# Sums of the attention and memory parts: the 13 that GpSimd made are made by VectorE at the same places

## The chip, the cores and the metric

The kernel runs on one core of a Trainium2 chip. A core has a matrix engine (TensorE, PE in the profile; its weight loads are PEld), a vector engine (VectorE, DVE), a scalar engine (ScalarE, ACT), a general engine (GpSimd, POOL) and a queue engine that issues the DMA transfers (SyncE, SP). Each works through its own list of instructions in order; semaphores tie the lists together. SBUF is the memory on the chip that all engines use, PSUM the eight banks into which PE writes. The metric is the time of one execution on the device in microseconds, the median of several runs.

## The reference

Two layers follow each other twice, on 2048 tokens of width 512: an attention layer with a memory, and a gated feed-forward layer. Both add to the tokens `x`.

```python
# attention: 32 heads of width 16, N = 4 segments of L = 512 tokens
q, k, v = x@wq, x@wk, x@wv              # x here is the layer norm of the tokens
for s in range(4):
    logits = einsum('bhqd,bhkd->bhqk', qs, ks) * scale + mask
    a_dot = einsum('bhqk,bhkd->bhqd', softmax(logits), vs)
    num = einsum('bhld,bhde->bhle', phi(qs), M)
    den = einsum('bhld,bhd->bhl', phi(qs), z)[..., None] + 1e-6
    o = g * num / den + (1 - g) * a_dot       # g = sigmoid(beta), one per head
    M, z = M + phi(ks)^T vs, z + sum(phi(ks))
x = x + concat(o) @ wo
# feed-forward, F = 1792
x = x + (gelu(norm(x) @ w_gate) * (norm(x) @ w_up)) @ w_down
```

`phi(t)` is `t + 1` above zero and `exp(t)` below. What this document is about is the sum in `o`: the attention part `(1 - g) * a_dot` plus the memory part `g * num / den`. In the first segment of each of the two attention layers the memory is empty and there is no sum.

## The kernel before

The work is cut into 8 steps `k`, four segments in each of the two rounds of layers. All weights and the tokens (`x_sb`) stay in SBUF. A step's work runs through the engines as follows. The names are those of tiles in the profile.

- PE makes `q`, `k` and `v` from the transposed, normalised tokens `xnT`; the results are copied out of PSUM (`ps`) to `q`, `kf`, `vaug`. `kx` holds masked copies of `kf`.
- PE makes scores (`ps<-q,kf`, `ps<-q,kx`); ACT takes the exponential into `pt` (L1864); the causal mask is laid on `pt` by POOL (L1813, and L1818 in two halves) or by DVE (L1823, a product with the triangle `tri`).
- PE multiplies `pt` with the values (`vaug`, `vz`). DVE turns the result round into `byq` (L1391), inverts the denominators `r` (L1401), scales to `ab` (L1407) and turns back into `aT` (L1414). `aT` now holds the attention part of one block of 8 heads: 128 rows by 512 tokens, bf16.
- For the memory, PE multiplies `phiq` with the state `mblk`; DVE scales to `am` (L1226); a DMA on SP's queue transposes `am` into `amT`. The state is kept in `macc` and `zacc` and spread into `mblk` by DVE (L1303, L1305, L1286). `phiq` and the keys' counterpart come from an exponential on ACT (L1147), a minimum `e` on DVE or POOL (L1170) and a sum on DVE (L1151).
- `aT` and `amT` are added into `aT` (L1417). This is the line that is changed. There are four blocks a segment and six segments with a memory, so 24 such sums.
- PE multiplies `aT` with `wo_sb`; DVE adds to `x_sb` (L1463), takes mean and variance (`st`, `mv`), and DVE or POOL normalises into `xn` (L920); a DMA transposes to `xnT`.
- The feed-forward part: `wg_sb`, gelu on ACT into `gel_sb`, `wu_sb`, the product on DVE (L1557), `wd_sb`, and a sum into `x_sb` (L1463).

The order of all this is worked out while the program is built. A planner keeps a clock for each engine, posts jobs with a time at which they are ready and a slack, and writes the instructions of each engine out in the order in which its clocks serve them. Some jobs may go to either of two engines: `on_dve_or_pool` (L712) posts such a job on DVE and, with a further slack, on POOL; the first of the two that is free takes it. The slack is `at_pool` for these sums and differs by stretches of 20 us of the planner's clock. In the built program POOL gets 13 of the 24 sums and DVE 11. The job's body, `add`, is handed the engine that took it.

Before a sum is posted, its `aT` must have been turned back and its `amT` must have landed by the planner's clock (`kept`, `put`). The instruction itself waits for the DMA's semaphore and for DVE's. After it stand the `wo_sb` products, which read `aT`, and the next step's `amT`, which reuses the tile.

Of the kernel before, what the change touches and what calls it, by code (L numbers as in the profile page):

```python
# [11 lines left out]
ALU = mybir.AluOpType  # L12
# [560 lines left out]
def order(pol, nc, cst, seg, wrk, psp, A_x, A_wq, A_wk, A_wv, A_wo, A_beta, B_x, B_w_gate, B_w_up, B_w_down, out):  # L573
# [138 lines left out]
    def on_dve_or_pool(ready, slack, later, fast, slow, emit, told):  # L712

        taken = []
        ck.dve.post(ready, slack, (fast, lambda: emit(nc.vector), told), taken=taken)
        if later is not None:
            ck.pool.post(ready, slack + later, (slow, lambda: emit(nc.gpsimd), told), taken=taken)
# [268 lines left out]
    class Att:  # L986
# [360 lines left out]
        def flush_item(self, flush, masked):  # L1347
            k = self.k
            u, b, h, n, pars, used = flush
# [6 lines left out]
            c0, c1 = (0, L) if h is None else (half * h, half * h + half)  # L1356
# [21 lines left out]
            def done():  # L1378
                for t in used:
                    slot = places[t]  # L1380
                    slot_users[slot] -= 1
                    if not slot_users[slot]:
                        slot_free[slot] = ck.made()
                flushed.append(number)
                if last:
                    ev["flushed", k] = ck.pe

                def turn():
                    if n == 0:
                        self.byq = wrk.tile([P, 2, TPS * 4, 32], F32, tag="byq", bufs=1, name="byq")  # L1390
                    nc.vector.transpose(out=(self.byq[:, pars[0], :, :].rearrange("p a c -> p (a c)") if h is None else  # L1391
                                             self.byq[:].rearrange("p u a c -> p (u a c)")[:, 0:2 * na * 32]), in_=ps()[:])

                def byq():
                    if h is None:
                        return self.byq[:]
                    return self.byq[:].rearrange("p u a c -> p (u a c)")[:, 0:2 * na * 32].rearrange("p (u a c) -> p u a c", u=2, c=32)

                def inverse():
                    self.r = wrk.tile([P, 2, TPS * 4, 1], F32, tag="pvr", bufs=1, name="r")  # L1400
                    nc.vector.reciprocal(out=self.r[:, :, 0:na, :], in_=byq()[:, :, :, DH:DH + 1])  # L1401

                made = []

                def scale():
                    made.append(seg.tile([P, TPS * 4, 32], BF16, tag=f"ab{unit % 2}", bufs=1, name="ab"))
                    nc.vector.tensor_tensor(out=made[0][:, 0:na, :].rearrange("p a (u d) -> p u a d", u=2),  # L1407
                                            in0=byq()[:, :, :, 0:DH],
                                            in1=self.r[:, :, 0:na, :].to_broadcast([P, 2, na, DH]), op=ALU.mult)

                def back():
                    if not self.aT:
                        self.aT = seg.tile([P, KT, L], BF16, tag="aT", bufs=1, name="aT")
                    nc.vector.transpose(out=self.aT[:, b, c0:c1], in_=made[0][:, 0:na, :].rearrange("p a c -> p (a c)"))  # L1414

                def add(eng):
                    eng.tensor_tensor(out=self.aT[:, b, c0:c1], in0=self.aT[:, b, c0:c1], in1=self.amT[b][:, c0:c1], op=ALU.add)  # L1417

                part = (c1 - c0) / L

                def turned(t):
                    on_dve_or_pool(t, slack, pol.at_pool, Port(0.15 + 0.275 * part), Port(0.16 + 1.0 * part, True), add, there)

                def there(t):
                    ev["turned", unit] = t
                    for i in range(2):
                        if h in (None, i):
                            ev["aTh", k, i, b] = t
                            self.halves[b] += 1
                    if self.halves[b] == 2:  # L1430
                        ev["aT", k, b] = t

                def kept(t):
                    ck.when(lambda: (k == 0 or ("wo", k - 1) in ev) and (self.s == 0 or ("amT", k, b) in ev), put)

                def put():
                    ck.dve.post(ck.pe, slack, (0.146 + 0.56 * part, back, turned if self.s else there))

                steps = [(0.71, turn, ps.read)]
                if 1 in pars:  # L1440
                    steps += [(0.155 + 0.2 * part, inverse, None), (Port(0.142 + 0.55 * part), scale, kept)]
                ck.dve.post(ck.made(), slack, *steps)
# [564 lines left out]
```

## Time and profile before

| | us |
|---|---|
| median of 3 runs | 536.3 (536.02 to 536.4) |
| the profiled execution, its own time | 536.81 |
| its span, first to last instruction | 535.1 |
| PE busy / DVE busy / ACT busy / POOL busy | 525.1 / 433.7 / 445.9 / 268.1 |

The granted clock of PE is 1.00 over the span. A row of the timeline is: start, duration, engine, line, operation, what is written and read, shape, how many are merged, and in brackets how long the engine sat idle before it and what ended that. A row of the chain of waits is start, duration and what. Instructions of one engine overlap a little at their ends, so the time that one takes from its engine is best read from its start to the next one's start.

### The profile page before, as it was taken

To read this page: it belongs to the slowest core of one execution; us is meant where nothing else is said; L and a number is where in the kernel's file an instruction comes from. 1 tells how busy PE (TensorE), PEld (TensorE's weight loads), DVE (VectorE), ACT (ScalarE), POOL (GpSimd) and SP (SyncE) were. 2 spreads that over 40 slices of the span, in tenths; PEclk is the share of its full clock that TensorE was granted. 3 is DMA by queue.
4 is the path that set the end of the run, shared out by engine and by line. 5 is a ranking of instruction groups with operands and counts; after the bars stand their busy time and mean duration, and the time that the engine had idled before them with its cause. 6 is when DMAs were issued, how large, how long until landed. Compare 5 with 4: busy or idle time off the path is not lost.

```text
span 535.1 us, 24177 instructions
## 1 busy us (share of the span) xinstructions
PE 525.1 (98%) x10697; PEld 276.3 (52%) x10697; DVE 433.7 (81%) x823; ACT 445.9 (83%) x598; POOL 268.1 (50%) x333
## 2 busy tenths in 40 slices
PE   9999989998999999999999999999999999999997
PEld 4454455444545454555564544555555456555554
DVE  6899996999997999879987788888977997586342
ACT  6999989887999989899898899799989988952320
POOL 2986472568541966528773366491654354500000
PEclk9999999999999999999999999999999999999999
DMA  8366940323231232201221113310260132102101
GB/s 268 76 121 139 215 141 4 69 41 73 44 60 24 49 55 42 33 12 25 51 44 31 25 24 32 61 34 1 52 103 3 33 51 52 24 2 51 33 2 41
DMA packets 76762, 29.99 MB, mean 56 GB/s; under 512 B 61042, under 2 KB 76658, under 8 KB 76658
## 3 DMA queue, kind: packets, MB, share of 16 engines
q1 hardware_dynamic: 76368, 28.20, 26.0%
q8 instruction: 83, 1.36, 1.0%
q10 hardware_dynamic: 290, 0.26, 0.1%
q14 instruction: 21, 0.17, 0.1%
HBM read 9.70 MB, written 2.10 MB: 22 GB/s over the span
## 4 chain that ended last, share of the span: by engine, by line
PE 77%; DVE 4%; ACT 3%; POOL 1%; issue 1%; DMA 0%; ACTq 0%
PE ps L541 77%; ACT pt L1864 1%; ACT gel_sb L1616 1%; POOL kx L726 1%; DVE xn L920 1%; ACT gel_sb L1519 1%; POOL e L1170 1%; ACT gel_sb L779 0%; DMA xnT<-xn 0%; DVE x_sb L1463 0%; DVE st L856 0%; DVE mblk L1286 0%; DVE byq L1391 0%; DVE x_sb L869 0%; ACT L1519 0%
## 5 line engine op out<-in xcount | busy, mean ns | idle before, releaser
L1864 ACT ACTIVATE pt<-ps 128x1024 bf16<-128x1024 f32 x288 | 278.9, 1036 | 26.8 <-PE ps L541 19.9
L1813 POOL TENSOR_SCALAR_AFFINE_SELECT pt<-pt 128x256 bf16<-128x256 bf16 (+1 forms) x192 | 113.6, 604 | 148.0 <-ACT pt L1864 145.6
L541 PE MATMUL ps<-xnT,wg_sb 128*32 128x512 bf16 (+3 forms) x1367 | 107.7, 362 | 0.3 <-DMA xnT<-xn 0.3
L541 PE MATMUL ps<-wd_sb,gel_sb 128*32 128x512 bf16 (+2 forms) x1431 | 106.1, 354 | 0.0
L541 PE MATMUL ps<-xnT,wu_sb 128*32 128x512 bf16 (+1 forms) x1252 | 103.6, 379 | 0.2 <-ACT gel_sb L1519 0.2
L1557 DVE TENSOR_TENSOR gel_sb<-gel_sb,ps 128x512 bf16<-128x512 bf16 x112 | 75.2, 683 | 30.8 <-PE ps L541 28.5
L541 PEld LDWEIGHTS <-gel_sb 128*32 128x32 bf16 (+1 forms) x1623 | 53.2, 97 | 41.2 <-issue 2.2
L541 PEld LDWEIGHTS <-wu_sb 128*32 128x32 bf16 (+1 forms) x1252 | 45.8, 97 | 45.3 <-issue 2.0
L541 PEld LDWEIGHTS <-wg_sb 128*32 128x32 bf16 (+1 forms) x1367 | 47.5, 97 | 38.7 <-issue 1.5
L1391 DVE STREAM_TRANSPOSE byq<-ps 128x512 f32<-128x512 f32 x64 | 45.4, 710 | 24.5 <-PE ps L541 23.8
L1170 POOL TENSOR_SCALAR e<-e 128x512 bf16<-128x512 bf16 x32 | 50.0, 1565 | 7.1 <-ACT e L1147 6.4
L1463 DVE TENSOR_TENSOR x_sb<-x_sb,ps 128x512 bf16<-128x512 bf16 (+1 forms) x54 | 34.0, 635 | 17.8 <-PE ps L541 17.7
L1818 POOL TENSOR_SCALAR_AFFINE_SELECT pt<-pt 64x1024 bf16<-64x1024 bf16 x32 | 38.1, 1192 | 17.8 <-ACT pt L1864 15.6
L541 PE MATMUL ps<-xnT,wk_sb 128*32 128x512 bf16 (+2 forms) x330 | 34.9, 377 | 0.7 <-ACT pt L1864 0.7
L541 PE MATMUL ps<-pt,vaug 128*32 128x256 bf16 (+2 forms) x1344 | 35.1, 239 | 0.1
L541 PE MATMUL ps<-wv_sb,xnT 128*32 128x512 bf16 (+1 forms) x227 | 32.4, 380 | 2.2 <-DVE x_sb L1463 1.8
L541 PE MATMUL ps<-xnT,wq_sb 128*32 128x512 bf16 (+2 forms) x339 | 34.0, 377 | 0.0
L1616 ACT ACTIVATE gel_sb<-gel_sb 128x1024 bf16<-128x1024 bf16 (+4 forms) x31 | 33.3, 1157 | 0.0
L541 PE MATMUL ps<-q,kx 32*128 32x64 bf16 (+2 forms) x1120 | 31.4, 217 | 0.6 <-ACT pt L1864 0.3
L541 PEld LDWEIGHTS <-vaug 128*32 128x32 bf16 x1344 | 27.2, 97 | 9.2 <-issue 1.6
L856 DVE BATCH_NORM_STATS2 st<-x_sb 128x6 f32<-128x512 bf16 x46 | 31.2, 679 | 0.4
L541 PEld LDWEIGHTS <-kx 32*128 32x128 bf16 x1120 | 16.8, 92 | 28.1 <-issue 27.4
(128 smaller groups left out, 722.1 us busy)
## 6 DMA issues: line engine op xcount, KB each, us to landing
vz<-vaug SPq DMA_DIRECT2D x14, 136.0 KB, 3.0
wg_sb<-in_B_w_gate_dram SPq DMA_DIRECT2D x8, 224.0 KB, 4.0
wu_sb<-in_B_w_up_dram SPq DMA_DIRECT2D x8, 224.0 KB, 3.9
wd_sb<-in_B_w_down_dram SPq DMA_DIRECT2D x7, 256.0 KB, 5.7
x_sb<-in_A_x_dram SPq DMA_DIRECT2D x3, 512.0 KB, 6.5
out_dram<-x_sb SPq DMA_DIRECT2D x12, 128.0 KB, 1.9
xnT<-xn SPq DMA_TRANSPOSE x56, 2.5
kx<-kf SPq DMA_DIRECT2D x12, 64.0 KB, 3.3
```

The costliest lines, as they stand in the source:

```text
L541: self.nc.tensor.matmul(*args, **kw)
L726: return lambda: eng.tensor_scalar(out=kx[:, :, C * which:C * which + n], in0=kf[:, :, 0:n], scalar1=masks[:, which:which + 1], scalar2=No ...
L856: nc.vector.bn_stats(out=self.st6[:, 0, :], in_=x_sb[:, self.tt0 + j, :])
L920: eng.tensor_scalar(out=xn[:], in0=x_sb[:, self.tt0 + j, :], scalar1=self.mv[:, j, 1:2] if self.wide else self.mv[:, j, 0:1], scalar2=self ...
L1170: lambda eng: eng.tensor_scalar(out=e[0][:], in0=e[0][:], scalar1=1.0, scalar2=None, op0=ALU.min), summed)
L1391: nc.vector.transpose(out=(self.byq[:, pars[0], :, :].rearrange("p a c -> p (a c)") if h is None else self.byq[:].rearrange("p u a c -> p ...
L1463: ck.dve.post(ck.made(), slack, (0.15 + 0.00104 * (c1 - c0), lambda: nc.vector.tensor_tensor(out=xt, in0=xt, in1=ps()[:, 0:c1 - c0], op=AL ...
L1557: ck.dve.post(ck.made(), NORMAL, (0.683, lambda: nc.vector.tensor_tensor(out=g, in0=g, in1=ps()[:], op=ALU.mult), lambda t: (ps.read(t), e ...
L1616: return (0.205 + 0.427 * (f1 - f0), lambda: nc.scalar.activation(out=g, in_=g, func=ACT.Gelu_apprx_tanh), lambda t: self.gelu_done(t, f0, ...
L1813: nc.gpsimd.affine_select(out=view, in_=view, pattern=[[0, 4], [0, n], [1, C]], compare_op=ALU.is_ge, fill=0.0, base=C, channel_multiplier=-1)
L1818: nc.gpsimd.affine_select(out=view, in_=view, pattern=[[0, 4 * TPS], [1, C]], compare_op=ALU.is_ge, fill=0.0, base=0, channel_multiplier=-1)
L1864: nc.scalar.activation(out=pt_all[:, s0:s0 + 2, 2 * p:2 * p + 2, :].rearrange("p r h c -> p h r c"), in_=ps_all[:, pair[0]:pair[1] + 1, :] ...
```

## The change

The body of the sum no longer uses the engine that it is handed, but always VectorE:

```diff
                 def add(eng):
-                    eng.tensor_tensor(out=self.aT[:, b, c0:c1], in0=self.aT[:, b, c0:c1], in1=self.amT[b][:, c0:c1], op=ALU.add)
+                    nc.vector.tensor_tensor(out=self.aT[:, b, c0:c1], in0=self.aT[:, b, c0:c1], in1=self.amT[b][:, c0:c1], op=ALU.add)
 
                 part = (c1 - c0) / L
```

The planner still books 13 of the sums on POOL's clock, so that every other instruction keeps its place in its engine's list. A sum that was booked on POOL is written into DVE's list behind what DVE had been given by then. Semaphore waits that named POOL name DVE instead. The lists of PE, ACT and SP are the same as before but for those waits.

The following rows show an engine's list in order; the shapes are written with their inner dimensions (`128x4x128` is 128 rows of 512). First POOL, at two sums of the second segment's four blocks (near 115 to 128 us in the profile). Before:

```order
L1813 AFFINE_SELECT pt<-pt 128x4x128
L1417 TENSOR_TENSOR aT<-aT,amT 128x512
L1170 TENSOR_SCALAR e<-e 128x512
L1813 AFFINE_SELECT pt<-pt 128x4x64 x2
L1813 AFFINE_SELECT pt<-pt 128x4x128
L920 TENSOR_SCALAR xn<-x_sb,mv,rs 128x512
L1813 AFFINE_SELECT pt<-pt 128x4x64 x2
L894 TENSOR_SCALAR ve<-mv 128x2
L899 TENSOR_TENSOR rs<-ve,mhalf 128x2
L1813 AFFINE_SELECT pt<-pt 128x4x128
L1417 TENSOR_TENSOR aT<-aT,amT 128x512
L1818 AFFINE_SELECT pt<-pt 64x1024 x2
```

And with the change:

```order
L1813 AFFINE_SELECT pt<-pt 128x4x128
L1170 TENSOR_SCALAR e<-e 128x512
L1813 AFFINE_SELECT pt<-pt 128x4x64 x2
L1813 AFFINE_SELECT pt<-pt 128x4x128
L920 TENSOR_SCALAR xn<-x_sb,mv,rs 128x512
L1813 AFFINE_SELECT pt<-pt 128x4x64 x2
L894 TENSOR_SCALAR ve<-mv 128x2
L899 TENSOR_TENSOR rs<-ve,mhalf 128x2
L1813 AFFINE_SELECT pt<-pt 128x4x128
L1818 AFFINE_SELECT pt<-pt 64x1024 x2
```

The minimum `e` and the half-masks of L1818 now follow a mask directly; the sums ahead of them are gone from this list.

DVE at the first of these two sums (near 115 us):

```order
 L1407 TENSOR_TENSOR ab<-byq,r 128x2x16x16
 L1414 STREAM_TRANSPOSE aT<-ab 128x512
+L1417 TENSOR_TENSOR aT<-aT,amT 128x512
 L1463 TENSOR_TENSOR x_sb<-x_sb,ps 128x512
 L1823 TENSOR_TENSOR pt<-pt,tri 128x1024
```

The sum stands right behind the transpose that makes its input, and ahead of a sum into `x_sb` and a mask product.

DVE near 395 us, in the third segment of the second attention layer:

```order
 L1414 STREAM_TRANSPOSE aT<-ab 128x512
 L1463 TENSOR_TENSOR x_sb<-x_sb,ps 128x512
+L1417 TENSOR_TENSOR aT<-aT,amT 128x512
 L1463 TENSOR_TENSOR x_sb<-x_sb,ps 128x256
 L1823 TENSOR_TENSOR pt<-pt,tri 128x1024
 L1414 STREAM_TRANSPOSE aT<-ab 128x512
 L1226 TENSOR_TENSOR am<-ps,rdm 128x512
+L1417 TENSOR_TENSOR aT<-aT,amT 128x512
 L1463 TENSOR_TENSOR x_sb<-x_sb,ps 128x256
 L778 CAST gel_sb<-ps 128x512
```

Two sums come in within a few instructions, each ahead of a half sum into `x_sb`.

## The prediction

> **What bounds the kernel now.** I read the page first, then the chain of waits, the waits of TensorE (PE) alone, the moved line, and last the timeline at the places where the moved instruction will stand.
>
> ```profile
> PE 525.1 (98%) x10697; PEld 276.3 (52%) x10697; DVE 433.7 (81%) x823; ACT 445.9 (83%) x598; POOL 268.1 (50%) x333
> 356.06 175.83 PE ps L541 x3787
> PE ps L541 <- DVE x_sb L1463: 1.8, 1, 1.8
> ```
>
> PE is busy for 525.1 of 535.1 us, and the chain runs on PE alone for the last 175.83 us of matmuls. A gain can come only from PE's few waits; the longest is one of 1.8 us, for VectorE (DVE). A loss comes wherever DVE becomes late for PE by more than PE's margin there. As hardly any wait is left to swallow it, I carry such lateness through to the end in full.
>
> ```profile
> L1417 POOL TENSOR_TENSOR aT<-aT,amT x13: 1152/1155/1165, 102.0 to 455.1; 128x512 bf16<-128x512 bf16 x13
> L1417 DVE TENSOR_TENSOR aT<-aT,amT x11: 383/615/1353, 101.7 to 481.0; 128x512 bf16<-128x512 bf16 x11
>   PEld L541: 0.2, 1
> ```
>
> Of the 24 sums, 13 run on GpSimd (POOL) at 1.155 us each, 15.0 us together; 11 run on DVE already. PE's weight loads idled behind a sum once, for 0.2 us. So the sums do not bound the kernel where they are. What counts is what their absence frees on POOL and what their presence delays on DVE.
>
> **The change part by part.** Removed: 13 POOL instructions. Added: the same 13 on DVE. PE, ACT and the DMA queue keep their order. Five of the 13 land where DVE has no idle time: one each at 102.0 (place A), 115.8 (B) and 126.5 (C), two at 395.4 and 398.0 (D). The other eight land at 155.6, 224.1, 225.7, 230.2, 339.4, 408.3, 422.5 and 453.5. The sum rows of two tables by stretch follow, first the four stretches of 3 us from A, B, C and D's first sum, then the eight stretches of 4 us from the other places (two of these overlap).
>
> ```profile
> sum 12.00, PE 12.00 PEld 5.81 DVE 11.96 ACT 9.38 POOL 11.01; mean PE 3.00 PEld 1.45 DVE 2.99 ACT 2.35 POOL 2.75
> sum 32.00, PE 32.00 PEld 17.05 DVE 25.91 ACT 30.18 POOL 18.67; mean PE 4.00 PEld 2.13 DVE 3.24 ACT 3.77 POOL 2.33
> ```
>
> In the eight, DVE is idle for 6.09 of 32 us, 0.76 a place, in gaps in which it waits for PE's products. A sum of about 0.35 us (next fence) fits into that, so I cost these eight at nothing. The cover is DVE's own idle time; were it gone, each place could cost up to 0.35 us.
>
> Place A first, with the price of one sum on DVE:
>
> ```profile
> 101.69 0.38 DVE L1417 TENSOR_TENSOR aT<-aT,amT 128x512 bf16<-128x512 bf16 x1
> 102.00 0.68 DVE L1557 TENSOR_TENSOR gel_sb<-gel_sb,ps 128x512 bf16<-128x512 bf16 x1
> 103.20 0.67 DVE L1557 TENSOR_TENSOR gel_sb<-gel_sb,ps 128x512 bf16<-128x512 bf16 x1
> 104.11 0.40 PE L541 MATMUL ps<-q,kx 32*128 32x64 bf16 x12
> 131.40 0.04 issue
> ```
>
> From a sum's start to the next instruction's is 102.00 - 101.69 = 0.31 us; by duration it is 0.38. I take 0.31 where the next instruction overlaps its end as here. PE's score matmul at 104.11 writes into the bank that the product of 103.20 reads until 103.87; 0.04 passes between a release and the start (the row of the chain). The margin is 104.11 - 103.87 - 0.04 = 0.20, so PE is late by 0.31 - 0.20 = **+0.1 us**, at most 0.2.
>
> Place B:
>
> ```profile
> 114.41 0.63 ACT L1147 ACTIVATE e<-q 128x512 bf16<-128x512 bf16 x1
> 115.08 0.71 DVE L1414 STREAM_TRANSPOSE aT<-ab 128x512 bf16<-128x512 bf16 x1
> 115.72 0.65 DVE L1463 TENSOR_TENSOR x_sb<-x_sb,ps 128x512 bf16<-128x512 bf16 x1
> 115.88 1.15 POOL L1417 TENSOR_TENSOR aT<-aT,amT 128x512 bf16<-128x512 bf16 x1 [0.30 <-DVE aT L1414]
> 116.29 1.29 DVE L1823 TENSOR_TENSOR pt<-pt,tri 128x1024 bf16<-128x1024 bf16 x1
> 116.97 0.40 PE L541 MATMUL ps<-q,kx 32*128 32x256 bf16 x12
> 117.00 1.93 POOL L1170 TENSOR_SCALAR e<-e 128x512 bf16<-128x512 bf16 x1
> 117.76 0.29 PE L541 MATMUL ps<-pt,vz 128*32 128x64 bf16 x16
> ```
>
> POOL has been free since 115.58 (idle for 0.30 before its sum), and its next work, the e of line 1170, has its input from ACT at 115.04. Without the sum it starts at about 115.6. The sum on DVE must wait for the transpose, which ends at 115.79, and starts at 115.82, so it will run while POOL works on e. What that does shows elsewhere:
>
> ```profile
> 249.86 1.48 POOL L1170 TENSOR_SCALAR e<-e 128x512 bf16<-128x512 bf16 x1
> 250.13 0.61 DVE L1417 TENSOR_TENSOR aT<-aT,amT 128x512 bf16<-128x512 bf16 x1
> 250.66 0.68 DVE L1463 TENSOR_TENSOR x_sb<-x_sb,ps 128x512 bf16<-128x512 bf16 x1
> 427.58 0.69 DVE L1823 TENSOR_TENSOR pt<-pt,tri 128x1024 bf16<-128x1024 bf16 x1
> ```
>
> There a sum that began 0.27 us into e took 250.66 - 250.13 = 0.53 to the next start. So x_sb starts at 115.82 + 0.53 = 116.35, 0.63 later than 115.72. It ended at 116.37 and PE started at 116.97: margin 0.56, so PE is late by **+0.1 us** (0.07). The mask product of line 1823 was held up by POOL's sum before (1.29 us, against 0.69 at 427.58). Now it starts 0.57 after x_sb, at 116.92, and ends at 117.61 against 117.58: the 0.03 lies within PE's 0.14 at 117.76. Bounds for B: nothing, if the sum takes 0.31; 1.1 us, if POOL's e holds it to the end (first rival).
>
> The Trainium skill, page "SBUF — State Buffer", section "Who interferes with whom", says that a DVE instruction with two SBUF inputs and a GpSimd one that reads SBUF exclude each other, and the later one fully blocks until the first ends. By that rule B would cost 1.1 us and not 0.1. The rows at 249.86 and 250.13 speak against it for e: the sum ended at 250.74, while e ran to 251.34.
>
> Place C, at PE's longest wait:
>
> ```profile
> 125.50 1.94 ACT L1864 ACTIVATE pt<-ps 128x1024 bf16<-128x1024 f32 x2 [0.24 <-PE ps L541]
> 126.61 1.15 POOL L1417 TENSOR_TENSOR aT<-aT,amT 128x512 bf16<-128x512 bf16 x1 [0.31 <-DVE aT L1414]
> 126.62 1.29 DVE L920 TENSOR_SCALAR xn<-x_sb,mv,rs 128x512 bf16<-128x512 bf16 x1
> 127.72 2.53 POOL L1818 TENSOR_SCALAR_AFFINE_SELECT pt<-pt 64x1024 bf16<-64x1024 bf16 x2
> 127.83 1.09 DVE L1305 TENSOR_TENSOR zacc<-zacc,zk 128x4 f32<-128x4 f32 x1
> 128.84 0.40 DVE L920 TENSOR_SCALAR xn<-x_sb,mv,rs 128x512 bf16<-128x512 bf16 x1
> 129.17 1.62 DVE L1286 TENSOR_TENSOR mblk<-macc,bd 128x512 bf16<-128x512 f32 x1
> 130.71 1.87 DVE L1463 TENSOR_TENSOR x_sb<-x_sb,ps 128x512 bf16<-128x512 bf16 x3
> 131.44 0.81 PE L541 MATMUL ps<-wv_sb,xnT 128*128 128x512 bf16 x3 [1.82 <-DVE x_sb L1463]
> ```
>
> DVE is held up three times here: the first xn takes 1.29 us (the second 0.40) and ends at 127.91, just after POOL's sum (127.76); zacc, four numbers a row, takes 1.09 and ends with the first half-mask of line 1818; mblk ends well after the second. Without its sum POOL starts the half-masks when ACT is done, 125.50 + 1.94 = 127.44, 0.28 us sooner than 127.72. DVE spends 0.31 on the sum, but then has the first xn in 0.33 instead of 1.21 (126.62 to 127.83), and is about at its second xn when the half-masks start. It is held up by these as before, 0.28 us sooner. x_sb, on which PE waits, comes 0.3 us earlier: **-0.3 us**. Bounds: nothing, if DVE's order of being held up changes for the worse; -1.3 in the second rival.
>
> Place D:
>
> ```profile
> 395.76 1.10 DVE L1823 TENSOR_TENSOR pt<-pt,tri 128x1024 bf16<-128x1024 bf16 x1
> 397.41 0.65 DVE L1226 TENSOR_TENSOR am<-ps,rdm 128x512 bf16<-128x512 f32 x1
> 397.85 1.16 POOL L1417 TENSOR_TENSOR aT<-aT,amT 128x512 bf16<-128x512 bf16 x1 [0.67 <-DMA amT<-am]
> 397.99 0.40 DVE L1463 TENSOR_TENSOR x_sb<-x_sb,ps 128x256 bf16<-128x256 bf16 x1
> 398.54 0.29 PE L541 MATMUL ps<-q,kx 32*128 32x64 bf16 x8
> ```
>
> The first sum costs 0.31 but takes from the mask product at 395.76 (1.10 us, against 0.69) the wait for POOL's sum: I count it as even, at worst +0.3. The second stands behind am, just ahead of the x_sb of 397.99; its DMA, on which it now makes DVE wait, has landed by 397.85. x_sb ends 0.31 later than 398.39, PE's margin at 398.54 is 0.11: **+0.2 us**, up to 0.5 with the first sum's 0.3.
>
> Sum: 0.1 + 0.1 - 0.3 + 0.2 = +0.1 us. On the profiled execution (span 535.1, its own time 536.81, 1.7 around the span) that gives a span of 535.2 and 536.9 us; its own time lies 0.5 above the median of 536.3, which becomes **536.4 us**.
>
> **The rivals.** First, slower: at B, POOL's e, started at 115.6, keeps the DVE sum out until its end at 115.6 + 1.48 = 117.08. x_sb then starts at 117.39 instead of 115.72, 1.67 later, and PE is late by 1.67 - 0.56 = 1.1 us: 0.1 - 0.1 + 1.1 gives 537.4, or 537.5 with the mask product behind it. For it: zacc at C stood still for a whole half-mask. Against it: the sum at 250.13. It decides as soon as e holds DVE for more than 1.0 us.
>
> Second, faster: at C, DVE gets its second xn in before the half-masks, so that only mblk meets them; mblk is then done 1 us sooner, between the two halves, and PE's 1.8 us wait shrinks by 1.3 in place of 0.3: 535.4. By the rows xn would come within 0.1 us of 127.44, so it is a close race.
>
> Third: DVE is so short of time that each of the 13 sums delays PE by its 0.36: 4.7 us, 541.0. Against it are the gaps in the eight stretches.
>
> That nothing is changed is excluded, since 13 instructions do change engines.
>
> **How the numbers follow.** About 0.2%, 1.1 us, is what a measurement can tell from no change here. The forecast, 536.4 (535.6 to 537.1 by A's 0.2, D's 0.5, B's and C's zeros and small shifts), has 0.64; the first rival 0.17, the second 0.12, the third 0.04, something unnamed 0.03. The range, 535.3 to 537.8, takes in the first two rivals. Faster by over 0.2% (below 535.2): the better part of the second rival, 0.09. Slower (above 537.4): the upper part of the first, the third and a rest, 0.2. Within: 0.71.
>
> **What would show it.** In the changed kernel's profile: 24 sums on DVE and none on POOL; POOL about 15 us less busy, DVE 4 to 7 us more, minus what it no longer waits for POOL at C; PE's wait for x_sb near 131 us at about 1.5; the sum near 115.8 at 0.5 to 0.7 us; a new PE wait of 0.2 near 398.5. I am wrong if that sum lasts over 1.2 us, if PE's wait near 131 vanishes or grows, or if PE waits for DVE at one of the eight places.

## The result, and the profile after

The changed kernel takes 535.01 us (median of 22 runs, 534.14 to 537.42), the kernel before 536.64 in the same series (22 runs, 535.73 to 538.03). The ratio is 0.9971, with a 95% interval of 0.9964 to 0.9979: 0.29% or 1.6 us faster. The forecast was 536.4, no change that can be told; the time lies 0.3 us under the range of 535.3 to 537.8. The profiled execution has a span of 533.3 us against 535.1. Here and below the ratio with its interval is a value of its own, not the quotient of the two medians, so the two can differ a little.

The page's busy times of the changed kernel:

```profile
PE 524.7 (98%) x10697; PEld 275.7 (52%) x10697; DVE 434.6 (81%) x836; ACT 445.8 (84%) x598; POOL 252.5 (47%) x320
```

The moved line, with its shortest, median and longest duration in ns:

```profile
L1417 DVE TENSOR_TENSOR aT<-aT,amT x24: 382/425/1351, 101.6 to 479.5; 128x512 bf16<-128x512 bf16 x24
```

And TensorE's (PE's) waits by what it waited for (us in all, times, longest):

```profile
PE ps L541 <- issue: 1.5, 2, 1.2
PE ps L541 <- DVE x_sb L1463: 0.4, 1, 0.4
PE ps L541 <- DMA xnT<-xn: 0.2, 1, 0.2
```

All 24 sums are on DVE. POOL lost 15.6 us of work and DVE gained 0.9 only, though it took over 13 sums: it is held up by POOL less. PE's wait for `x_sb`, 1.8 us before, is 0.4.

Where the time came from is read by setting each of PE's 10697 matmuls against the same one of the kernel before. PE's shift is the start of a matmul less the start of the same one before; below zero it is earlier. It changes at few places, given here at the times of the kernel before:

| place in the kernel before | change of PE's shift, us | forecast |
|---|---|---|
| start to 76.2 | -0.11 | not spoken of |
| A, 104 to 106 | +0.13 | +0.1 |
| B, 117 | +0.11 | +0.1 |
| C, 131.44 | **-1.40** | **-0.3** |
| 144.6 to 145.7 | +0.18 | not spoken of |
| 199.8 to 203.8 | -0.55 | not spoken of |
| D, 398.55 | +0.14 | +0.2 |
| 422.84 | -0.10 | 0 |

With 0.09 more in small steps, PE's last matmul starts 1.51 us earlier; the other 0.3 of the span lie behind it, where the output leaves. At 144.62 PE comes before a transposing DMA has landed, and gives back a part; at 199.78 a like wait, 0.3 us before, is absent.

Place C after the change, DVE, POOL and PE in the timeline (start, duration, engine, line, operation; in brackets the idle time and what ended it):

```profile
126.70 0.42 DVE L1417 TENSOR_TENSOR aT<-aT,amT 128x512 bf16<-128x512 bf16 x1
127.04 0.28 DVE L1303 TENSOR_TENSOR macc<-macc,ps 128x128 f32<-128x128 f32 x1
127.24 0.41 DVE L920 TENSOR_SCALAR xn<-x_sb,mv,rs 128x512 bf16<-128x512 bf16 x1
127.56 0.16 DVE L1305 TENSOR_TENSOR zacc<-zacc,zk 128x4 f32<-128x4 f32 x1
127.63 1.31 DVE L920 TENSOR_SCALAR xn<-x_sb,mv,rs 128x512 bf16<-128x512 bf16 x1
127.66 2.89 POOL L1818 TENSOR_SCALAR_AFFINE_SELECT pt<-pt 64x1024 bf16<-64x1024 bf16 x2 [1.21 <-ACT pt L1864]
128.87 0.67 DVE L1286 TENSOR_TENSOR mblk<-macc,bd 128x512 bf16<-128x512 f32 x1
129.46 1.87 DVE L1463 TENSOR_TENSOR x_sb<-x_sb,ps 128x512 bf16<-128x512 bf16 x3
130.19 1.46 PE L541 MATMUL ps<-wv_sb,xnT 128*128 128x512 bf16 x6 [0.42 <-DVE x_sb L1463]
```

The two half-masks of line 1818 are one group here; the first ends at 128.79 and the second starts at 128.86. The second xn is held until the first half-mask ends (1.31 us, against 0.41 for the first xn). At the border mblk gets in together with it and takes 0.67 us. In the kernel before, zacc was held by the first half-mask, the second xn got in at the border, and mblk was held by the second one for 1.62 us. So x_sb starts at 129.46 instead of 130.71. One hold costs what it did before, about 0.9 us; what changed is how many there are, and which instruction stood at DVE's head when the half-masks began.

### The profile page after: what moved, and what is told of

It reads as the page before. It is cut to its first block, busy times and chain, and to the rows that moved or that the text cites. A ratio compares the mean times of both kernels' runs of the same rounds, so it can differ in the third digit from the quotient of the medians.

```text
span 533.3 us, 24180 instructions
## 1 busy us (share of the span) xinstructions
PE 524.7 (98%) x10697; PEld 275.7 (52%) x10697; DVE 434.6 (81%) x836; ACT 445.8 (84%) x598; POOL 252.5 (47%) x320
## 4 chain that ended last, share of the span: by engine, by line
PE 75%; DVE 5%; ACT 3%; POOL 1%; issue 1%; DMA 1%; ACTq 0%
PE ps L541 75%; ACT pt L1864 1%; DVE xn L920 1%; DVE st L856 1%; ACT gel_sb L1616 1%; POOL kx L726 1%; DVE x_sb L1463 1%; ACT gel_sb L1519 1%; POOL e L1170 1%; DMA xnT<-xn 1%; ACT gel_sb L779 0%; DVE ab L1407 0%; DVE byq L1391 0%; DVE aT L1414 0%; DVE x_sb L869 0%
## 5 line engine op out<-in xcount | busy, mean ns | idle before, releaser
L1813 POOL TENSOR_SCALAR_AFFINE_SELECT pt<-pt 128x256 bf16<-128x256 bf16 (+1 forms) x192 | 112.4, 598 | 176.4 <-ACT pt L1864 173.9
L1818 POOL TENSOR_SCALAR_AFFINE_SELECT pt<-pt 64x1024 bf16<-64x1024 bf16 x32 | 38.5, 1203 | 20.7 <-ACT pt L1864 17.4
```

The lines of the kernel that those rows point to most:

```text
L1813: nc.gpsimd.affine_select(out=view, in_=view, pattern=[[0, 4], [0, n], [1, C]], compare_op=ALU.is_ge, fill=0.0, base=C, channel_multiplier=-1)
L1818: nc.gpsimd.affine_select(out=view, in_=view, pattern=[[0, 4 * TPS], [1, C]], compare_op=ALU.is_ge, fill=0.0, base=0, channel_multiplier=-1)
```

## The experiments

Theory 1: the gain is made at C alone, by taking holds of DVE by POOL off the path to x_sb; the other twelve sums cost 0.3 us or nothing. Rivals: the gain is the relief of POOL or the earlier product in aT for PE, wherever the sums stand; or durations on DVE simply add up, with no part played by the half-masks' borders. Each edit is to the kernel before unless said otherwise; (k, b) == (1, 3) is the sum at C.

**One sum moved, or the other twelve.**

```diff
-                    eng.tensor_tensor(out=self.aT[:, b, c0:c1], in0=self.aT[:, b, c0:c1], in1=self.amT[b][:, c0:c1], op=ALU.add)
+                    (nc.vector if (k, b) == (1, 3) else eng).tensor_tensor(out=self.aT[:, b, c0:c1], in0=self.aT[:, b, c0:c1], in1=self.amT[b][:, c0:c1], op=ALU.add)
```

> Only the sum at 126.6 us (place C) goes to VectorE; the other 12 stay on GpSimd. Theory 1, the whole gain is made at C, where GpSimd's sum kept VectorE from its small instructions: PE's wait near 131 us falls from 1.8 to about 0.4 us, and without the delays at A, B and D (0.1 us each) the kernel is 1.5 to 2.0 us faster than before. Rival, the gain comes from GpSimd being relieved of 15 us in all: one of 13 sums gives a thirteenth of it, 0.1 us, and nothing measurable.

Measured: 535.57 us against 537.02, ratio 0.9963 (0.9940 to 0.9985). PE's shift at C is -1.40, and there is none at A, B or D.

```diff
-                    eng.tensor_tensor(out=self.aT[:, b, c0:c1], in0=self.aT[:, b, c0:c1], in1=self.amT[b][:, c0:c1], op=ALU.add)
+                    (eng if (k, b) == (1, 3) else nc.vector).tensor_tensor(out=self.aT[:, b, c0:c1], in0=self.aT[:, b, c0:c1], in1=self.amT[b][:, c0:c1], op=ALU.add)
```

> The 12 other sums go to VectorE; the one at 126.6 us (place C) stays on GpSimd. Theory 1: slower than before by the 0.3 to 0.4 us that PE lost at A, B and D, and PE's wait near 131 us is 1.8 as before. Rival (relief of GpSimd in all): nearly the whole gain of 1.5 us stays.

Measured: 536.49 against the same 537.02, ratio 0.9985 (0.9956 to 1.0014): the time itself tells nothing, and the 0.3 to 0.4 us that were expected to be lost lie within its interval. PE's shifts do tell: +0.13 at A, +0.11 at B, +0.13 at D, none at C. PE's wait there, first in the kernel with one sum moved, then in that with the other twelve:

```profile
PE ps L541 <- DVE x_sb L1463: 0.4, 1, 0.4
```

```profile
PE ps L541 <- DVE x_sb L1463: 1.8, 1, 1.8
```

The one sum makes the gain. Twelve sums taken off POOL bring none, so POOL's relief as such is not it.

**The sum at C left out.** This kernel leaves that one sum of the attention and memory parts out altogether.

```diff
-                    eng.tensor_tensor(out=self.aT[:, b, c0:c1], in0=self.aT[:, b, c0:c1], in1=self.amT[b][:, c0:c1], op=ALU.add)
+                    (k, b) == (1, 3) or eng.tensor_tensor(out=self.aT[:, b, c0:c1], in0=self.aT[:, b, c0:c1], in1=self.amT[b][:, c0:c1], op=ALU.add)
```

> As before, but the sum at 126.6 us is left out altogether, so that block's memory part is missing from the output: neither engine makes it. It shows what the 0.31 us on VectorE costs once GpSimd's hold is gone. If the hold of GpSimd's sum is the cause, the gain is that of moving the sum or more: 1.5 to 2.1 us, and VectorE has its second xn done before the half-masks. If it is the later start of the wo products that counts, the gain is the same as with the sum on VectorE to 0.1 us.

Measured: 534.62 against 537.02, ratio 0.9943 (0.9909 to 0.9978); by the medians that is 2.4 us, more than expected, though the interval takes the expected gain in. PE's shift at C is -1.98 and its wait is gone. The timeline there (this execution runs 2 us late, by a stop of PE near 76 us, of which more at the end):

```profile
129.16 0.41 DVE L920 TENSOR_SCALAR xn<-x_sb,mv,rs 128x512 bf16<-128x512 bf16 x1
129.49 0.68 DVE L1286 TENSOR_TENSOR mblk<-macc,bd 128x512 bf16<-128x512 f32 x1
129.51 2.87 POOL L1818 TENSOR_SCALAR_AFFINE_SELECT pt<-pt 64x1024 bf16<-64x1024 bf16 x2 [1.05 <-ACT pt L1864]
130.36 1.88 DVE L1463 TENSOR_TENSOR x_sb<-x_sb,ps 128x512 bf16<-128x512 bf16 x3 [0.19 <-PE ps L541]
```

Without the sum even mblk gets in, 0.02 us ahead of the half-masks, and x_sb waits only for its product from PE. The lead alone does not decide this: in the changed kernel the second xn started 0.03 us ahead of them and was held. The 0.34 us that the sum costs DVE at C (126.70 to 127.04 in the changed kernel) are thus worth 0.6 us of PE's time: 1.98 against 1.40.

**The whole change, with POOL still held.** Here POOL makes the sum at C once more, into a tile that nothing reads, after DVE's.

```diff
-                    nc.vector.tensor_tensor(out=self.aT[:, b, c0:c1], in0=self.aT[:, b, c0:c1], in1=self.amT[b][:, c0:c1], op=ALU.add)
+                    nc.vector.tensor_tensor(out=self.aT[:, b, c0:c1], in0=self.aT[:, b, c0:c1], in1=self.amT[b][:, c0:c1], op=ALU.add); (k, b) == (1, 3) and nc.gpsimd.tensor_tensor(out=junk[:], in0=self.aT[:, b, c0:c1], in1=self.amT[b][:, c0:c1], op=ALU.add)
```

> All 13 sums on VectorE as in the change, but at 126.6 us GpSimd makes a second copy of the sum into a tile that nobody reads, after VectorE's, so that it is busy as before and PE does not wait for it. Theory 1 (GpSimd's sum holds VectorE up, and pushes the half-masks back): the gain at C is gone, PE's wait near 131 is 1.8 to 2.3 us, and the kernel is at 536.9 to 537.6, slower than before by up to 1. Rival (PE has aT sooner for the wo products, and that is the gain): the wait stays at 0.4 and the kernel at 535.0.

Measured: 537.94 against 537.02, ratio 1.0001 (0.9977 to 1.0026). The median lies above the 536.9 to 537.6 expected, while the ratio shows no difference from the kernel before. The gain is gone, and the timeline shows the holds of the kernel before, one after the other:

```profile
127.04 1.16 POOL L1417 TENSOR_TENSOR junk<-aT,amT 128x512 bf16<-128x512 bf16 x1 [0.77 <-DVE aT L1417]
127.07 1.28 DVE L920 TENSOR_SCALAR xn<-x_sb,mv,rs 128x512 bf16<-128x512 bf16 x1
128.27 1.09 DVE L1305 TENSOR_TENSOR zacc<-zacc,zk 128x4 f32<-128x4 f32 x1
129.28 0.40 DVE L920 TENSOR_SCALAR xn<-x_sb,mv,rs 128x512 bf16<-128x512 bf16 x1
129.60 1.62 DVE L1286 TENSOR_TENSOR mblk<-macc,bd 128x512 bf16<-128x512 f32 x1
131.87 1.46 PE L541 MATMUL ps<-wv_sb,xnT 128*128 128x512 bf16 x6 [2.49 <-DVE x_sb L1463]
```

PE's wait, 2.49 us, is longer than the 1.8 to 2.3 expected: POOL's sum starts only behind DVE's, at 127.04 against 126.61 before. The input of PE's product, aT, was ready as early as in the changed kernel, and it brought nothing: the earlier product as a cause falls. A POOL instruction of 1.16 us at that place holds the first xn, and with it shifts who is held next.

**mblk later, without and with the sum moved.** If x_sb is late because mblk is held ahead of it, then to issue mblk behind the three additions into x_sb (line 1463) must gain with every sum left on POOL. The edit keeps mblk back until the third of them:

```diff
-    ev["start"] = 0.0
+    ev["start"] = 0.0; kept_back, passed = [], []; release = lambda: kept_back and (passed.append(1) or len(passed) < 3 or kept_back.pop()())
...
-                ck.dve.chain(ck.made(), pol.mem_slack, *first, (Port(0.69), spread, None), (Port(0.2), z, told))
+                ck.dve.chain(ck.made(), pol.mem_slack, *first, (Port(0.69), spread if k != 1 else lambda: kept_back.append(spread), None), (Port(0.2), z, told))
...
-                ck.dve.post(ck.made(), slack, (0.15 + 0.00104 * (c1 - c0), lambda: nc.vector.tensor_tensor(
-                    out=xt, in0=xt, in1=ps()[:, 0:c1 - c0], op=ALU.add), lambda t: (ps.read(t), told(t))))
+                ck.dve.post(ck.made(), slack, (0.15 + 0.00104 * (c1 - c0), lambda: (nc.vector.tensor_tensor(
+                    out=xt, in0=xt, in1=ps()[:, 0:c1 - c0], op=ALU.add), release()), lambda t: (ps.read(t), told(t))))
```

> Edit: no sum is moved at all; only mblk (L1286) at 129.17 is issued behind the x_sb additions that used to follow it. Theory (the wait of PE that the change shortened was mblk held up by the second half-mask): x_sb follows the second xn at about 129.2 instead of 130.71, PE's wait near 131 is 0.3 us instead of 1.8, and the time is about 1.5 us below the kernel before, with every sum where it was. Rival (the relief of GpSimd by its sum is what gains; or x_sb is held in mblk's place): the wait stays at 1.4 to 1.8 us, and no gain.

Measured: 535.65 against 537.22, ratio 0.9953 (0.9931 to 0.9975). No sum is moved, and PE's wait falls to 0.26 us:

```profile
127.74 2.54 POOL L1818 TENSOR_SCALAR_AFFINE_SELECT pt<-pt 64x1024 bf16<-64x1024 bf16 x2
127.86 1.09 DVE L1305 TENSOR_TENSOR zacc<-zacc,zk 128x4 f32<-128x4 f32 x1
128.87 0.40 DVE L920 TENSOR_SCALAR xn<-x_sb,mv,rs 128x512 bf16<-128x512 bf16 x1
129.19 1.87 DVE L1463 TENSOR_TENSOR x_sb<-x_sb,ps 128x512 bf16<-128x512 bf16 x3
129.92 1.46 PE L541 MATMUL ps<-wv_sb,xnT 128*128 128x512 bf16 x6 [0.26 <-DVE x_sb L1463]
```

The additions run beside the second half-mask at their usual 1.87 us for three: they are not held. The Trainium skill, page "SBUF — State Buffer", section "Who interferes with whom", says that a DVE instruction with at most one SBUF input, outside its two-port modes, does not contend with GpSimd; x_sb has one input in SBUF and one in PSUM, and the rows agree. PE's shift at C is -1.56, a little more than the change's -1.40. But by 140 PE has given 0.68 of it back: mblk now stands ahead of the statistics of x_sb, and the four xn that follow from them come only 0.83 earlier than in the kernel before (135.68 against 136.51; in the changed kernel 1.25). The span of this trace is 534.3 us, 0.8 below the kernel before, less than the median of the runs suggests.

> Edit: only the sum at 126.5 (place C) is moved to VectorE, and mblk (L1286) of that place is issued behind the x_sb additions (L1463) that used to follow it. Theory (x_sb, on which PE waits, stands behind whatever VectorE instruction GpSimd's half-masks hold up): x_sb follows the second xn directly, at about 128.9 instead of 129.46, PE's wait near 131 goes from 0.4 us to about 0, and the time is 1.8 to 2.0 us below the kernel before, 0.4 below the kernel with that one sum moved (1.4). If instead the three x_sb are now held up by the second half-mask in mblk's place (rival: whatever stands third is held), x_sb ends at about 130.5, the wait is 1.5 us, and nothing is gained.

Both edits together: 535.46 against 537.22, ratio 0.9972 (0.9949 to 0.9995). At C the expectation held: x_sb follows the second xn directly, PE's wait is gone, and its shift is -1.98. The 2 us were not kept whole, and the time cannot be told from that of the kernel with the one sum moved. Some 0.73 go back between 138 and 140 in the same way, and in the profiled execution PE loses another 3.5 us near 200, first to a wait for a transposing DMA and then in slow matmuls (32 in 1.88 us, where the 32 of the same form just before took 1.06):

```profile
197.85 2.93 SPq L754 DMA_TRANSPOSE xnT<-xn  x2
199.36 1.88 PE L541 MATMUL ps<-xnT,wg_sb 128*32 128x256 bf16 x32 [2.25 <-DMA xnT<-xn]
```

In the kernel before, the matmuls at this place waited 0.3 us (at 199.78), in the changed one not at all. Why it took 2.25 in this execution wasn't tried.

> Edit: the whole change (all 13 sums on VectorE), and mblk of place C issued behind the x_sb additions, as in the kernel that moved mblk alone. Theory: PE's last wait of 0.4 us near 131 goes, so PE is 1.8 to 2.0 us earlier there than in the kernel before; but mblk now delays VectorE's statistics behind it, as in the two other kernels with mblk later, where PE lost 0.7 us again between 138 and 141, so at 145 PE is only 0.9 to 1.3 us ahead and the time is the changed kernel's to 0.3 either way (1.3 to 1.9 below the kernel before). Rival (what is won at PE's wait is kept): PE still 1.8 us or more ahead at 145, and the time 2.0 to 2.3 us below the kernel before.

The whole change with mblk later: 535.78 against 536.77, ratio 0.9984 (0.9966 to 1.0002), so not shown to be better than the change. PE's shift at C is -1.98, of which 0.47 is lost by 140; at 145 PE is 1.2 us ahead of the kernel before, as expected.

**The sum at C moved, and made twice on DVE.** This puts a few tenths of a microsecond more on DVE just ahead of the half-masks; by the theory that costs not these tenths, but another order of holds.

```diff
-                    eng.tensor_tensor(out=self.aT[:, b, c0:c1], in0=self.aT[:, b, c0:c1], in1=self.amT[b][:, c0:c1], op=ALU.add)
+                    (nc.vector if (k, b) == (1, 3) else eng).tensor_tensor(out=self.aT[:, b, c0:c1], in0=self.aT[:, b, c0:c1], in1=self.amT[b][:, c0:c1], op=ALU.add); (k, b) == (1, 3) and nc.vector.tensor_tensor(out=junk[:], in0=self.aT[:, b, c0:c1], in1=self.amT[b][:, c0:c1], op=ALU.add)
```

> Edit: only the sum at 126.5 is moved to VectorE, and made a second time behind it, into a tile that nothing reads: 0.33 us more on VectorE just ahead of the half-masks. Theory (two instructions pass per border between GpSimd's instructions, so what counts is which instruction stands where when the half-masks begin): now the first xn is held by the first half, zacc passes with it, and the second xn is held by the second half; mblk and x_sb come after it, x_sb at about 130.9 and PE's wait 1.8 to 2.2 us: the 1.4 us gain goes whole, and the time is that of the kernel before to 0.4 slower. Rival (durations simply add up): 0.33 of the 1.35 is lost, PE's wait 0.75, time 1.0 us below the kernel before.

Measured: 537.09 against 537.22, ratio 0.9991 (0.9970 to 1.0011). This execution runs 1.2 us late ahead of C.

```profile
127.72 0.42 DVE L1417 TENSOR_TENSOR aT<-aT,amT 128x512 bf16<-128x512 bf16 x1
128.18 0.43 DVE L1417 TENSOR_TENSOR junk<-aT,amT 128x512 bf16<-128x512 bf16 x1
128.52 0.28 DVE L1303 TENSOR_TENSOR macc<-macc,ps 128x128 f32<-128x128 f32 x1
128.64 2.36 POOL L1818 TENSOR_SCALAR_AFFINE_SELECT pt<-pt 64x1024 bf16<-64x1024 bf16 x2 [1.18 <-ACT pt L1864]
128.72 1.21 DVE L920 TENSOR_SCALAR xn<-x_sb,mv,rs 128x512 bf16<-128x512 bf16 x1
129.85 0.14 DVE L1305 TENSOR_TENSOR zacc<-zacc,zk 128x4 f32<-128x4 f32 x1
129.92 1.24 DVE L920 TENSOR_SCALAR xn<-x_sb,mv,rs 128x512 bf16<-128x512 bf16 x1
131.08 0.67 DVE L1286 TENSOR_TENSOR mblk<-macc,bd 128x512 bf16<-128x512 f32 x1
132.40 1.02 PE L541 MATMUL ps<-wv_sb,xnT 128*128 128x512 bf16 x4 [1.56 <-DVE x_sb L1463]
```

The order of holds is the one expected: the first xn is held, zacc gets in at the border, the second xn is held again. PE's wait is 1.56 us (expected 1.8 to 2.2) and its shift at C -0.26. From the first sum's start to macc's DVE takes 0.80 us, against 0.34 with one sum, so the second costs it 0.46 (0.33 was expected). These 0.46 us cost 1.1 us of the gain; if durations added up, PE's wait would be 0.4 + 0.46, about 0.9. That the shift is not quite zero was my sizing: the second half-mask was shorter here than I had reckoned (the two take 2.36 us, against 2.53 in the kernel before).

## Why the prediction was wrong

The step that failed is **the term for place C, -0.3 us; it measured -1.40**. The mechanism around it was right: DVE is held up there by POOL, and x_sb, on which PE waits, comes earlier when the sum leaves POOL. The sentence that failed is that DVE "is held up by these as before, 0.28 us sooner". The half-masks did begin sooner, at 127.66 against 127.72; as all engines run 0.15 us later here by the delays at A and B, that is 0.2 us sooner as DVE counts. But they did not hold DVE as before: it had by then done the first xn and begun zacc (127.56). So the line of instructions stood one further: the second xn took zacc's place as the one held, mblk took xn's place at the border, and nothing was left for the second half-mask to hold, as the additions into x_sb ran beside it in their usual 1.87 us. Three holds became one. Before, the first xn took 0.88 us, zacc 0.93 and mblk 0.95 more than they take undisturbed (0.41, 0.16 and 0.67 in the rows after); now only the second xn takes 0.90 more. That is 1.86 less, of which the sum and the short gap ahead of it take back about 0.45: the -1.40. The forecast had the first of the three holds going, but let the half-masks swallow what that gives. I had written down in the rows of before that zacc ended "with the first half-mask" and that mblk ended after the second, but had not asked who goes in between.

The second rival had the size, -1.3 and 535.4 us, and mblk at the border. Its condition was not met as put: the second xn started 0.03 us ahead of the half-masks and was held all the same (1.31 us). It was enough that one instruction fewer stood in the line. I gave it 0.12 because I thought that the close race at 127.44 decided. Close it was; in the kernel with the change and mblk later the second xn did get in:

```profile
127.73 0.41 DVE L920 TENSOR_SCALAR xn<-x_sb,mv,rs 128x512 bf16<-128x512 bf16 x1
127.82 2.52 POOL L1818 TENSOR_SCALAR_AFFINE_SELECT pt<-pt 64x1024 bf16<-64x1024 bf16 x2 [1.29 <-ACT pt L1864]
```

But the changed kernel lost the race and made the gain, so the race was not what decided. That the rival's number came out so near is in part luck, as its way there was another.

The other terms, by PE's shift and by the kernel with twelve sums moved:

- A: +0.1 forecast, +0.13 measured (and with twelve sums). Right.
- B: +0.1 forecast, +0.11 measured (and with twelve sums). The row that I took from 250.13 gave the duration, 0.61 us, exactly:

```profile
115.58 1.48 POOL L1170 TENSOR_SCALAR e<-e 128x512 bf16<-128x512 bf16 x1
115.86 0.61 DVE L1417 TENSOR_TENSOR aT<-aT,amT 128x512 bf16<-128x512 bf16 x1
116.39 0.67 DVE L1463 TENSOR_TENSOR x_sb<-x_sb,ps 128x512 bf16<-128x512 bf16 x1
116.99 0.68 DVE L1823 TENSOR_TENSOR pt<-pt,tri 128x1024 bf16<-128x1024 bf16 x1
117.00 0.51 PE L541 MATMUL ps<-q,kx 32*128 32x256 bf16 x12
```

- The first rival, that POOL's e keeps the sum out to its end at B, falls with these rows: the sum ended at 116.47, e at 117.06. The rule of the Trainium skill's page "SBUF — State Buffer", section "Who interferes with whom", that the later one blocks until the first ends, does not describe e; it does describe the half-masks at C, where the second xn ended at 128.94, just after the first half-mask (128.79), but for the order: by the rows xn had started 0.03 us ahead of it.
- D: +0.2 forecast, +0.14 measured (+0.13 with twelve sums). Right.
- The eight places at nothing: no shift over 0.1 us at any. Right, though one of these sums (at 452.02) was held to 0.89 us by a half-mask: PE had the room for it. The third rival, 0.36 per sum, falls with that.
- Not in the sum: 0.18 given back at 145 and 0.55 gained near 200, both by transposing DMAs that PE meets a little earlier or later. With the start's -0.11 they are a further -0.5 us, of the size of the scatter between executions.

With C at -1.40 in place of -0.3 my own sum would have been -1.0 us, 535.3 us on the median that I took: at the edge of the range, and 0.3 us above the time. The rest is the -0.5 us that no term of mine spoke of.

## What to carry to other kernels

Where one engine's instructions hold up another's, don't price a moved instruction by its duration: write down the line of instructions that stands at the held engine when each holding one begins, before and after the move, and see which one on the critical path ends up behind a hold. A few tenths of a microsecond can be worth over a microsecond there, or nothing. A wait that is shortened in that way pays only until the next one that was hidden, so a second edit at the same place (mblk later) won 0.6 us at C and kept none that the times can tell.

## What the runs showed of the hardware

- **Two go at a border, or one.** At C, in every trace in which the first half-mask held a DVE instruction and the second followed it (0.06 to 0.07 us between them), the one that was held and the next one both got in before the second half-mask held DVE again: zacc and xn in the kernel before, xn and mblk after the change, xn and zacc in the kernel with the sum twice. The instruction at the border runs at its undisturbed 0.40 or 0.67 us and, in the change, costs the second half-mask time instead: that one took 1.68 us, the first 1.13. It is no general rule. Where POOL's sum at C was followed by a half-mask without a gap (127.76 and 127.72 in the kernel before), only the held xn went, and zacc was held. And elsewhere in the changed kernel two sums on DVE were held by two half-masks in a row (0.82 and 1.35 us for the two), with the same 0.06 us between the masks:

```profile
343.80 2.42 POOL L1818 TENSOR_SCALAR_AFFINE_SELECT pt<-pt 64x1024 bf16<-64x1024 bf16 x2
344.39 2.09 DVE L1417 TENSOR_TENSOR aT<-aT,amT 128x512 bf16<-128x512 bf16 x2
```

At C the next instruction started no later than 0.01 us after the second half-mask, here the second sum started 0.13 after it. That this is the reason is not shown.
- **POOL's e holds only at first.** An undisturbed sum takes 0.38 us. The sums at 115.86 after the change (0.61) and at 250.13 before (0.61) end as if they had begun 0.51 and 0.50 us after e did, though e goes on for another 1 us. The sum at 101.69 before, which began 1.16 us into an e (100.53 to 102.01), took its undisturbed 0.38. So these rows show a hold at e's start alone; no run varied e, so the reason stays open.
- **A stop of PE that varies.** Near 76 us PE stops for a time in which it waits for nothing that the profile shows: 0.99 us in the trace before, 1.24 after, none in two of the experiments' traces and up to 1.71 in the others; PE's shift changed there by -1.1 to +2.4 us, slow matmuls behind the stop taken in. It lies ahead of all moved sums. Single executions of one kernel can differ by more than the change is worth, so PE's shift at a place, set against the shift just ahead of it, was the sharper measure here than the time.
- **The clock after a wait.** The slow matmuls near 200 us in the kernel with both edits are a lower granted clock, and the sum-left-out kernel shows the same behind its stop near 76 us. Two stretches of 2 us, ahead of and behind the wait, first of the former, then of the latter (length, busy time of PE, PEld, DVE, ACT and POOL, granted clock, DMA share, GB/s):

```profile
195.00:197.00 2.00, 2.00 (x86) 1.63 (x84) 1.97 (x6) 2.00 (x4) 1.79 (x4) 1.00 0.66 134
199.30:201.30 2.00, 1.94 (x36) 1.32 (x36) 1.31 (x3) 0.62 (x2) 1.05 (x2) 0.53 0.59 117
```

```profile
73.00:75.00 2.00, 1.98 (x42) 0.85 (x31) 2.00 (x5) 2.00 (x4) 1.40 (x3) 1.00 0.92 287
76.60:78.60 2.00, 1.91 (x25) 0.75 (x29) 0.08 (x1) 1.53 (x2) 1.86 (x2) 0.63 0.09 29
```

The clock fell to 0.53 after a wait of 2.25 us and to 0.63 after a stop of 1.71; each cost PE about another 1.5 us. It stayed at 1.00 after the wait of 2.49 at C in the kernel with POOL held, after the 1.82 of the kernel before, and after a stop of 1.66 near 76 us in the kernel with the sum twice. So the length of the wait alone does not decide it, and what does wasn't tried.
